# Opening order, zero matmuls and load queues of a fused attention and MLP-mixer kernel

## The chip, the cores and the metric

The kernel runs on one core of one Trainium2 chip. The metric is the device time of one execution in microseconds; all times below are microseconds unless another unit stands beside them. The core has a matmul engine (PE), three engines for elementwise work (DVE, ACT, POOL), and SP, which here only issues transfers. Each works through its own queue in order and waits on semaphores for the others.

## The reference

Four batches of 8 heads, 768 positions and head size 64 go through attention with a sliding window of 128 and four sink keys, and the result through one block of an MLP-mixer with `d_tok` 256 and `d_ch` 1536. All inputs are fp32.

```python
keep = is_sink | in_window                    # first 4 keys, or 0 <= query - key < 128
scores = where(keep, (q @ k.T) / sqrt(D), -1e9)
x = (softmax(scores) @ v), heads side by side # [B, 768, 512]
u = x + (relu(x.T @ w_tok1) @ w_tok2).T
out = u + relu(u @ w_ch1) @ w_ch2
```

## The kernel before

**Tiling.** The 32 heads form eight groups of four: g = 0 to 7, two groups to a batch. Work is cut into named operations, and the names are used in this document. `Lq2.0`, `Lk2.0`, `Lv2.0` load q, k and v of group 2. q and k come as bf16 through a casting transfer issued by POOL; v comes as fp32 through a plain transfer issued by SP and is cast on POOL by `Cv2` into the tile `va`. `Tq2.0` and `Tk2.0` are 32x32 block transposes on DVE that bring q and k into the form the scores need. `SC2.0`, `SC2.1`, `SC2.2` are score matmuls for three pairs of key tiles, `EX` the exponentials on ACT, `MK` the multiplications by a 0/1 mask on DVE, `KZ`, `SK`, `EXK` the same path for the sink keys, `PV2.0` to `PV2.5` the products with v for six tiles of 128 queries, and `XB` the division by the sum, which writes the tile `x_b` and frees the matmul's bank.

The mixer of a batch needs both of its groups: `T1` (with `w_tok1`), `H1` (ReLU), then `T2` (with `w_tok2`), `U` (adds x), `X` and `UTE` (u transposed) or, for half of batch 0, `TT` and `UE`, which make the transposed u directly; then 24 tiles of `C1` (with `w_ch1`), `V` (ReLU), `C2` in three quarters of the inner dimension at a time (with `w_ch2`), `O` (adds u) and the store `ST`. In a name such as `C10.03` the first digit after the operation is the batch.

**Order.** The instructions are written out in an order that a small planner in the kernel computes, `order_of` (line 65). It gives each operation an assumed duration, an assumed landing time for transfers, and picks on each engine what can start first, priorities breaking ties. The list `FIRST` (line 19) gives priorities and engines to the operations of the opening, that is groups 0 and 1 and the first mixer up to the first channel matmuls. The order on each engine is then fixed; only semaphores decide the times.

**What the edit touches.** Group 0's q and k are loaded in two pieces (`PIECES`, line 321): the first piece of each as fp32 by SP, cast by `Ck0.0` on DVE and `Cq0.0` on ACT (lines 345 to 353), the second by casting transfers on POOL (lines 354 to 357). On SP, v of groups 0 and 1 follows. `weight` (line 724) issues the weights on POOL: `tok1`, `tok2`, four pieces of `ch1`, two of `ch2`. v of groups 2 and 3 is held back by a semaphore until the piece `ch1.3` has landed (`gate`, line 366). The buffers for q and k are two deep (`bfp`, line 187), those for raw v three deep (`stage`, line 186), so later loads also wait for their buffers. POOL handles its casts and its transfers in one queue: a load that stands behind a cast waits with it.

**Zero matmuls.** Where the planner sees PE idle before the time `Filler.until` (line 766), it puts in matmuls of the zero tile `warm` into a free bank (lines 110 to 118 and 763 to 774), each 128x512. The tile itself is zeroed on DVE (line 247).

**Masks.** For the pairs listed in `PEM` (line 320) the mask is added on PE by two matmuls of `ident` with `mneg`, and no `MK` follows.

Of the kernel before, what the change touches and what calls it, by code (L numbers as in the profile page):

```python
# [19 lines left out]
MK0.00:D UE0.03:A PV1.3:P vs1:G XB0.1:D SK1:P C10.03:P C10.02:P Tq0.1:D Lv0.0:S Tk1.0:D PV1.5:P XB1.2:D  # L20
EX1.20:A Lk0.1:G blk:G SC1.02:P SC1.00:P SC1.22:P Lq0.1:G Tq0.0:D V0.01:D XB0.3:D first:G vsink:D Lk1.0:G
PV0.0:P EX0.11:A va:G Lk0.0:S V0.02:A T10.014:P zero:D Lq0.0:S XB0.2:D Cq0.0:A MK1.0256:D ident:G Wch2.1:G
T10.104:P Wtok2:G Cv1:G Wch1.1:G MK1.10:D MK0.0256:D T10.114:P EX0.10:A EX0.21:A mnegs:D KZ1:D EX1.00:A SK0:P
C10.00:P EX1.01:A XB1.0:D EX0.01:A MK0.10:D Tk0.1:D EX0.00:A Lq1.0:G Cv0:G PV0.1:P T10.004:P TT0.01:P SC1.12:P
EX1.21:A XB0.5:D MK0.20:D ones:D XB0.0:D V0.00:A H10.00:A Wch1.0:G SC1.10:P SC1.20:P Wch2.0:G PV0.2:P Ck0.0:D
PV1.0:P EX0.20:A PV1.1:P H10.01:A XB1.4:D KZ0:D H10.10:A Tk0.0:D Wch1.3:G rest:G SC0.20:P MK1.00:D H10.11:D
UE0.02:A TT0.00:P UE0.01:A T10.110:P EX1.11:A Lv1.1:S Tq1.0:D PV0.5:P EX1.10:A vsl:G EXK0:A PV1.2:P mneg:G
EXK1:A Wch1.2:G V0.03:D PV0.4:P SC0.22:P SC0.10:P SC0.00:P SC0.02:P PV1.4:P T10.100:P kz:D first1:D SC0.12:P
Wtok1:G TT0.02:P PV0.3:P T10.010:P UE0.00:A XB0.4:D C10.01:P Lv1.0:S TT0.03:P T10.000:P
# [10 lines left out]
class Op:  # L40


    n = 0

    def __init__(self, name, engines, emit, deps=(), pri=0, rows=False, take=(), free=(), land=0.0, dear=None):
        self.name, self.engines, self.emit = name, engines, emit
        self.deps, self.pri, self.rows = [d for d in deps if d is not None], pri, rows
        self.take, self.free, self.land, self.dear = take, free, land, dear or {}
        self.dmas = 1 if land else 0
        self.far = 0.0  # L50
        self.begin = self.end = self.engine = self.made = None
        Op.n += 1
        self.seq = Op.n
# [11 lines left out]
def order_of(ops, slots, filler):  # L65
# [3 lines left out]
    dma_free, rows = {"SP": 1.9, "POOL": 3.4, "ACT": 1.9}, False  # L69
# [8 lines left out]
    def start(op, e):  # L78
        t = free_at[e]
        for d in op.deps:  # L80
            t = max(t, d.end + lag(d, op, e))
        if op.take:
            for kind in {p.kind for p in op.take}:
                n = sum(p.kind == kind for p in op.take)
                t = max(t, sorted(banks[kind])[n - 1])
        if op.dmas:
            t = max(t, flying[e][-9 + op.dmas])
        if e == "PE" and op.rows != rows:
            t += 0.095
        return t  # L90

    while waiting:
        best = None
        ready = [o for o in waiting if all(d.end is not None for d in o.deps)]
        per = {}
        for o in ready:
            at = {e: start(o, e) for e in o.engines}
            soonest = min(at[e] + o.engines[e] + o.dear.get(e, 0) for e in at)
            for e, t in at.items():
                if t < INF and t + o.engines[e] + o.dear.get(e, 0) <= soonest + 1e-9:  # L100
                    per.setdefault(e, []).append((t, o))
        for e, c in per.items():
            first = min(t for t, _ in c)
            t, o = min(((t, o) for t, o in c if t <= first + 0.2), key=lambda x: (x[1].pri, -x[1].far, x[1].seq))
            if best is None or t < best[0]:
                best = (t, e, o)
        if best is None:
            raise RuntimeError("stuck: " + ", ".join(o.name for o in waiting[:20]))
        t, e, o = best
        idle = t - free_at["PE"] - 0.3  # L110
        kind, i = min(((k, i) for k in banks for i in range(slots[k])), key=lambda x: banks[x[0]][x[1]])
        if e == "PE" and filler.until > t and idle > 0.3 and banks[kind][i] < free_at["PE"] - 0.3:
            f = filler.make(kind, i, int(idle / 0.22) + 1)
            f.begin, f.engine = free_at["PE"], "PE"
            f.end = banks[kind][i] = f.begin + f.engines["PE"]
            done.append(f)
            rows = False
            t = max(t, f.end + 0.095 * (o.rows != rows))
        o.begin, o.engine = t, e
        free_at[e] = t + o.engines[e]  # L120
        if e == "PE":
            rows = o.rows
        if o.land:
            dma_free[e] = max(dma_free[e], t + (2.5 if e == "POOL" else 1.4)) + o.land
            o.end = dma_free[e] + 0.9
            flying[e] += [o.end] * o.dmas
        else:
            o.end = free_at[e]
        for p in o.take:
            p.slot = min(range(len(banks[p.kind])), key=lambda i: banks[p.kind][i])  # L130
            banks[p.kind][p.slot] = INF
        for p in o.free:
            p.left -= 1
            if p.left == 0:
                banks[p.kind][p.slot] = free_at[e] + 0.07
        done.append(o)
        waiting.remove(o)
# [12 lines left out]
def kernel(  # L150
# [144 lines left out]
    def c_vsink(e):  # L295
        nc.vector.memset(vsink, 0.0)  # L296
# [23 lines left out]
    PEM = ((1, 2),)  # L320
# [9 lines left out]
    def load_ops(g, deps, vdeps, pri, gate=None):  # L330
# [6 lines left out]
        for n, (w, c) in enumerate([(w, c) for c in range(C) for w in "qk"]):  # L337
# [7 lines left out]
            if g == 0 and c == 0:  # L345
                def plain(e, w=w, src=src):
                    raws[w] = stage.tile([P, R, D], FP32, name="raw_" + w, bufs=1)
                    nc.sync.dma_start(out=raws[w], in_=src)

                def cast(e, w=w, bf=bf):  # L350
                    copy_on[e](bf(), raws[w])
                o = op(f"L{w}{g}.{c}", ("SP", 0.46), plain, [], pri + n, land=land)
                o = op(f"C{w}{g}.{c}", {"ACT": act(R * D), "DVE": dve(R * D, 2)}, cast, [o], pri)
            else:
                def casting(e, src=src, bf=bf):
                    nc.gpsimd.dma_start(out=bf(), in_=src)
                o = op(f"L{w}{g}.{c}", ("POOL", 0.56), casting, deps + (prev.dt[w] if prev else []), pri + n, land=land)
            G.load[w].append(o)
        parts = 2 if g == 1 else 1
        for x in range(parts):  # L360
# [7 lines left out]
            G.load["v"].append(op(f"Lv{g}.{x}", ("SP", 0.46), vv, vdeps, pri + 2, land=GH * S * D * 4e-6 / BWV / parts))  # L368


    def attention(g, xb, base):
# [31 lines left out]
        veng = {"POOL": 1.02e-3 * N}  # L403
        G.cv = [op(f"Cv{g}", veng, castv, G.load["v"] + [c_va_op] + old, -5 if g < 2 else base + 2)]

        def sinkkeys(e):
# [5 lines left out]
        G.kz = op(f"KZ{g}", ("DVE", 0.12), sinkkeys,  # L412
                  G.dt["k"] + [c_kz_op, c_blk_op] + ([prev.sk] if prev else []), base + 1)
# [42 lines left out]
        def masks(u, ex):  # L456
# [3 lines left out]
            for lo, hi, m in ((0, 256, mfirst), (256, 512, mrest)) if u == 0 else ((0, 512 if u == 1 else 384, mrest),):  # L460
# [4 lines left out]
                r.append(op(f"MK{g}.{u}{lo}", ("DVE", dve(4 * (hi - lo), 2)), mask, ex + [c_first_op, c_rest_op], base + u))  # L465
# [237 lines left out]
    c_ident_op = op("ident", ("POOL", 0.6), c_ident, (), -200)  # L703
# [4 lines left out]
    o_vs = op("vsink", ("DVE", 1.2), c_vsink, (), -140)  # L708
# [6 lines left out]
    for o in groups[0].load["v"] + groups[1].load["v"]:  # L715
        o.deps += groups[1].load["k"][-1:]
    o_vsl = op("vsl", ("POOL", 2.6), c_vsink_load, [o_vs], -150, land=0.2)
    o_vsl.dmas = 4
    c_vsink_op = op("vs1", ("POOL", 0.6), c_vsink_one, [o_vs, o_vsl], -60)
# [4 lines left out]
    def weight(key, dst, src, deps, pri, run):  # L724

        def emit(e):
            w_ops[key].made = nc.gpsimd.dma_start(out=dst, in_=src)
        w_ops[key] = op("W" + (key if isinstance(key, str) else f"{key[0]}.{key[1]}"), ("POOL", 0.9), emit, deps, pri, land=dst.shape[0] * dst.shape[1] / 16 * run * 1e-3)
        return w_ops[key]

    weight("tok1", w_tok1, moe_w_tok1.rearrange("(t p) n -> p t n", p=P), [groups[0].load["v"][0]], -40, 60)
    weight("tok2", w_tok2, moe_w_tok2.rearrange("(t p) n -> p t n", p=P), [groups[1].load["v"][0]], -40, 135)
    qf = DCH // 4
    c1w = [weight(("ch1", i), w_ch1[:, :, ts(i, qf)], moe_w_ch1.rearrange("(t p) n -> p t n", p=P)[:, :, ts(i, qf)],
                  [groups[1].load["v"][0]], -40 + i, 78) for i in range(4)]
    c2src = moe_w_ch2.rearrange("(t p) n -> p t n", p=P)
    weight(("ch2", 0), w_ch2[:, 0:8], c2src[:, 0:8], [c1w[0]], -30, 96)
    weight(("ch2", 1), w_ch2[:, 8:12], c2src[:, 8:12], [c1w[0]], -29, 96)
# [5 lines left out]
    for b in range(B):  # L744
        batches[b].x = X(batches[b - 2].u if b >= 2 else [])
        for a in range(GB):
            g = GB * b + a
            if g >= 2:
                deps = [c1w[3]] if g < 4 else []
                load_ops(g, deps, deps + groups[g - 2].cv, 1000 * b - 700, c1w[3] if g < 4 else None)  # L750
# [12 lines left out]
    class Filler:  # L763


        until = 36.0

        @staticmethod
        def make(kind, i, n):
            def emit(e):  # L770
                t = psum[kind][i].tile([P, 512], FP32, name="ps_warm", tag="b")
                for _ in range(n):
                    nc.tensor.matmul(t, warm[:, 0:P], warm, start=True, stop=True)  # L773
            return Op("dummy", {"PE": 0.22 * n}, emit)
# [37 lines left out]
```

## Time and profile before

| | us |
|---|---|
| median of 6 runs | 220.1 (218.75 to 221.13) |
| profiled execution, its own time | 219.4 |
| span of its instructions | 217.7 |
| PE busy | 202.9 (93%) |
| DVE busy | 132.5 (61%) |
| ACT busy | 101.6 (47%) |
| POOL busy | 34.2 (16%) |
| chain that ended last: PE | 87% of the span |

The span runs from the first to the last instruction of the program; the execution's own time holds 1.7 more around it. Times in views of the trace count from the start of the span. In a line of the merged timeline stand the start, the length, the engine, the source line, the operation, what it writes and reads, how many instructions were merged, and in brackets the engine's idle time before it and what ended that. A line of the stretches view holds the stretch, its length, the busy time and number of instructions of PE, PE's weight loads, DVE, ACT and POOL, the granted PE clock, the share of the DMA engines and GB/s by bytes as written. A line on a transfer ends with its size and the time from issue to landing.

### The profile page before, as it was taken

Reading aid. Unit: us, or ns where it says so; the run is one execution under the profiler, and the core shown is the slowest. Engines: PE = TensorE matmul, PEld = TensorE weight load, DVE = VectorE, ACT = ScalarE, POOL = GpSimd, SP = SyncE. Lnnn points to the kernel's source line nnn. Section 1 sums busy time; section 2 is a strip of 40 time slices with the busy share of each in tenths; the row PEclk is TensorE's granted clock in tenths of the full one; section 3 lists DMA queues with packets and bytes.
Section 4 is the critical chain, followed back from the end, with each engine's and each line's share of the span. In section 5 each row is a group of like instructions: output and inputs, shape, how many; then the busy total and the mean of one; then the engine's idle time right before and its main releaser. Section 6 shows DMA issues by size and latency. Waiting matters only on the chain.

```text
span 217.7 us, 4148 instructions
## 1 busy us (share of the span) xinstructions
PE 202.9 (93%) x1744; PEld 116.1 (53%) x1764; DVE 132.5 (61%) x232; ACT 101.6 (47%) x170; POOL 34.2 (16%) x57
## 2 busy tenths in 40 slices
PE   0995999999989999998999999999999999999993
PEld 0442577655546564546765544566755545555552
DVE  7658895259669999999998812589664122001131
ACT  2116765553496511599925320799514301753300
POOL 7919810002260220012000000000000000000000
PEclk9999699999999999999999999999999999999999
DMA  6996999999999955193001013100001113001122
GB/s 175 229 218 90 204 203 197 204 210 230 220 219 235 255 144 118 53 144 76 3 0 48 0 59 114 72 3 3 0 0 51 48 50 114 32 2 48 48 97 99
DMA packets 36243, 23.49 MB, mean 108 GB/s; under 512 B 26112, under 2 KB 31232, under 8 KB 36224
## 3 DMA queue, kind: packets, MB, share of 16 engines
q0 software_dynamic: 7616, 9.85, 26.5%
q1 hardware_dynamic: 28608, 13.37, 25.2%
q8 instruction: 14, 0.23, 0.4%
q14 instruction: 5, 0.04, 0.1%
HBM read 26.77 MB, written 6.29 MB: 152 GB/s over the span
## 4 chain that ended last, share of the span: by engine, by line
PE 87%; DVE 7%; ACT 3%; issue 1%; DVEq 0%
PE ps_v L645 28%; PE ps_w L667 28%; PE ps_s L435 6%; PE ps_warm L773 5%; PE ps_h L560 4%; PE ps_u L612 4%; PE ps_o L511 3%; DVE pT L463 3%; ACT pT L452 2%; PE ps_o L516 2%; PE ps_ut L622 2%; PE ps_o L508 2%; PE ps_k L489 1%; DVE kz L407 1%; DVE vsink L296 1%
## 5 line engine op out<-in xcount | busy, mean ns | idle before, releaser
L645 PE MATMUL ps_v<-uT,w_ch 128*128 128x384 bf16 x384 | 68.0, 326 | 0.7 <-ACT uT L227 0.5
L667 PE MATMUL ps_w<-w_ch,v 128*128 128x512 bf16 (+1 forms) x287 | 65.1, 370 | 0.6
L231 ACT ACTIVATE v<-ps_v 128x384 bf16<-128x384 f32 x86 | 42.1, 493 | 45.0 <-PE ps_v L645 33.9
L452 ACT ACTIVATE pT<-ps_s 128x1024 bf16<-128x1024 f32 (+1 forms) x48 | 43.3, 953 | 28.9 <-PE ps_s L435 26.1
L645 PEld LDWEIGHTS <-w_ch 128*128 128x128 bf16 x384 | 36.4, 98 | 25.4 <-issue 1.4
L677 DVE TENSOR_TENSOR o<-ps_w,u_sb 128x512 f32<-128x512 f32 (+1 forms) x25 | 16.8, 670 | 51.4 <-PE ps_w L667 49.4
L667 PEld LDWEIGHTS <-v 128*128 128x128 bf16 x300 | 28.7, 98 | 29.6 <-issue 0.2
L463 DVE TENSOR_TENSOR pT<-pT,mrest 128x1024 bf16<-128x1024 bf16 (+2 forms) x23 | 22.0, 960 | 3.9 <-ACT pT L452 3.7
L617 DVE TENSOR_TENSOR u_sb<-ps_u,x_b 128x512 bf16<-128x512 f32 x24 | 15.1, 682 | 10.8 <-PE ps_v L645 5.1
L532 DVE TENSOR_TENSOR x_b<-ps_o,rc 128x256 bf16<-128x256 f32 (+1 forms) x45 | 19.9, 442 | 1.5
L226 POOL CAST va<-raw_v 128x1536 bf16<-128x1536 f32 x8 | 11.8, 1473 | 47.0 <-DMA raw_v<-in_v_dram 26.9
L435 PE MATMUL ps_s<-qT,kT 32*128 32x256 bf16 (+1 forms) x384 | 17.7, 269 | 1.5 <-ACT pT L452 1.4
L385 DVE STREAM_TRANSPOSE qT<-qb 128x768 uint32<-128x768 uint32 (+1 forms) x9 | 16.4, 1873 | 1.8 <-DMA qb<-in_q_dram 1.8
L511 PE MATMUL ps_o<-va,pT 128*128 128x65 bf16 x192 | 16.7, 197 | 0.7 <-DVE h L233 0.3
L385 DVE STREAM_TRANSPOSE kT<-kb 128x768 uint32<-128x768 uint32 (+1 forms) x9 | 16.8, 1885 | 0.0
L773 PE MATMUL ps_warm<-warm 128*128 128x512 bf16 x43 | 11.8, 433 | 5.2 <-DVE warm L247 5.1
L435 PEld LDWEIGHTS <-kT 32*128 32x128 bf16 x384 | 9.9, 94 | 11.1 <-issue 9.9
L511 PEld LDWEIGHTS <-pT 128*128 128x128 bf16 x192 | 14.0, 99 | 3.0 <-DVE h L233 0.6
L516 PE MATMUL ps_o<-va,pT 128*128 128x65 bf16 x160 | 15.1, 195 | 0.0
L227 ACT ACTIVATE uT<-ps_ut 128x512 bf16<-128x512 bf16 (+1 forms) x13 | 7.3, 564 | 13.0 <-PE ps_ut L622 12.6
L560 PE MATMUL ps_h<-x_b,w_tok 128*128 128x256 bf16 x96 | 12.1, 273 | 0.0
L516 PEld LDWEIGHTS <-pT 128*128 128x128 bf16 x160 | 11.6, 99 | 0.8 <-issue 0.4
(60 smaller groups left out, 136.0 us busy)
## 6 DMA issues: line engine op xcount, KB each, us to landing
out_dram<-o SPq DMA_DIRECT2D x23, 256.0 KB, 2.0
raw_v<-in_v_dram SPq DMA_DIRECT2D x7, 768.0 KB, 11.7
kb<-in_k_dram POOLq DMA_DIRECT2D x7, 384.0 KB, 10.2
qb<-in_q_dram POOLq DMA_DIRECT2D x7, 384.0 KB, 7.9
w_ch<-in_moe_w_ch_dram POOLq DMA_DIRECT2D x4, 384.0 KB, 8.7
w_ch<-in_moe_w_ch_dram POOLq DMA_DIRECT2D x1, 1024.0 KB, 18.5
raw_v<-in_v_dram SPq DMA_DIRECT2D x2, 384.0 KB, 12.5
w_tok<-in_moe_w_tok_dram POOLq DMA_DIRECT2D x2, 384.0 KB, 5.6
```

What stands on the lines that cost most here:

```text
L231: nc.scalar.activation(o, i, AF.Relu)
L385: nc.vector.transpose(G.T[w].rearrange("p s x -> p (s x)").bitcast(UINT32).rearrange("p (i r) -> p r i", i=Q)[:, r], G.bf[w][:, r].bitcast ...
L435: nc.tensor.matmul(bank[h][:, at:at + w], G.T["k"][r, ts(kt, P), db], G.T["q"][r, ds(kt * P, w), db], start=not pem and db == 0, stop=db = ...
L452: nc.scalar.activation(o, i, AF.Exp, scale=scale)
L463: nc.vector.tensor_tensor(out=t, in0=t, op=ALU.mult, in1=m[:, 0:hi - lo].rearrange("p (o x) -> p o x", o=1).to_broadcast([P, GH, hi - lo]))
L511: nc.tensor.matmul(ps[:, h], G.pT[qt // 2][:, h, ds(256 * (qt % 2), P)], G.va[:, h, qt], start=(qt < 2 and h == 0), stop=(h == GH - 1 and ...
L516: nc.tensor.matmul(ps[:, h], G.pT[kt // 2][:, h, ds(256 * (kt % 2) + P, P)], G.va[:, h, kt], start=False, stop=(h == GH - 1), skip_group_c ...
L532: nc.vector.tensor_tensor(out=xb.tile[:, ds(q0, n), c0:c0 + W].rearrange("p n (h d) -> p n h d", h=GH), in0=ps[:, :, :, 0:D], in1=rc.to_br ...
L560: nc.tensor.matmul(p.tile, w_tok1[:, t, ts(tt, P)], xb.tile[:, t, ds(a * W, W)], start=(t == 0), stop=(t == NT - 1))
L645: nc.tensor.matmul(ps, w_ch1[:, c, ts(ft, P)], M.uT[hf][:, c], start=(c == 0), stop=(c == NC - 1))
L667: nc.tensor.matmul(p.tile, M.v1t[hf][:, ft, ts(st % NH, P)], w_ch2[:, ft, ds(lo, n)], start=(ft == 0), stop=(ft == NF - 1))
L773: nc.tensor.matmul(t, warm[:, 0:P], warm, start=True, stop=True)
```

## The change

- **Order list.** `FIRST` is replaced by another list. On DVE `warm` comes first; the zeroing of `vsink` goes to ACT; all casts of group 0's q and k go to ACT; the cast of v of group 0 goes from POOL to DVE.
- **First loads.** Both pieces of group 0's q and k are plain fp32 transfers on SP, in the order k piece 1, q piece 0, k piece 0, q piece 1, ahead of v. On POOL the memsets and selects for `va`, `blk`, `ident` and `mneg` come ahead of the casting loads of group 1's k and q. The ones in `vsink` are written before its four small transfers instead of after them.
- **Masks.** The pair (0, 0) joins `PEM`, so group 0's first mask is added on PE.
- **Zero matmuls.** The first block has 24 of 128x512 instead of 38. Later gaps before time 29.0 of the plan are filled with 128x128 ones, 19 in three places, instead of six of 128x512 in two.
- **Weights.** `tok1` waits by a semaphore for v of group 0; the other weights follow it in a row on POOL, with the cast of v of group 1 between the second and the third piece of `ch1`, and all come ahead of q and k of groups 2 and 3 (which are planned in this order too: q2, q3, k2, k3). The eight pieces had come as `ch1.1`, `ch1.0`, `ch1.3`, `ch1.2`, `ch2.1`, `ch2.0`; now they come in the order of their numbers.
- **Planner.** It now keeps DVE and POOL operations marked `port` apart in time, holds some operations behind the placing of others (`follows`), and has other assumed durations. So the order of the later batches changes as well: for instance `Tq4.0` stands on DVE directly behind `XB2.3` instead of behind `XB3.5` and `O0.40`, the scores `SC2.0` stand two `C1` tiles sooner on PE, and `Tq7.0` stands ahead of `U2.0` instead of behind `UTE2.4`.

```diff
-    dma_free, rows = {"SP": 1.9, "POOL": 3.4, "ACT": 1.9}, False
+    dma_free, rows = {"SP": 1.9, "POOL": 6.0, "ACT": 1.9}, None
...
+        for d in op.follows:
+            t = max(t, d.begin + d.engines[d.engine])
...
+        if e in op.port:
+            t = max(t, port)
...
-        idle = t - free_at["PE"] - 0.3
+        idle = t - free_at["PE"] - (1.0 if rows is None else 0.15)
...
-        if e == "PE" and filler.until > t and idle > 0.3 and banks[kind][i] < free_at["PE"] - 0.3:
-            f = filler.make(kind, i, int(idle / 0.22) + 1)
+        if e == "PE" and filler.until > t and idle > 0.15 and banks[kind][i] < free_at["PE"] - 0.2:
+            f = filler.make(kind, i, idle, rows is None, o.rows)
...
     def c_vsink(e):
-        nc.vector.memset(vsink, 0.0)
+        nc.scalar.activation(vsink.rearrange("p g h x -> p (g h x)"), warm[:, 0:1].to_broadcast([P, NG * GH * D1]), AF.Copy)
...
-    PEM = ((1, 2),)
+    PEM = ((0, 0), (1, 2))
...
-            if g == 0 and c == 0:
-                def plain(e, w=w, src=src):
-                    raws[w] = stage.tile([P, R, D], FP32, name="raw_" + w, bufs=1)
-                    nc.sync.dma_start(out=raws[w], in_=src)
+            if g == 0:
+                def plain(e, w=w, c=c, src=src):
+                    raws[w, c] = stage.tile([P, R, D], FP32, name=f"raw_{w}{c}", bufs=1)
+                    nc.sync.dma_start(out=raws[w, c], in_=src)
...
+            if g in (2, 3):
+                o.follows = [w_ops["ch2", 1]]
...
-        veng = {"POOL": 1.02e-3 * N}
+        veng = {"POOL": 0.96e-3 * N}
+        if g < 2:
+            veng |= {"DVE": dve(N, 2), "ACT": act(N)}
...
-    for o in groups[0].load["v"] + groups[1].load["v"]:
-        o.deps += groups[1].load["k"][-1:]
...
+    for o in groups[1].load["q"] + groups[1].load["k"]:
+        o.deps += [c_ident_op, o_mneg, c_blk_op]
...
             w_ops[key].made = nc.gpsimd.dma_start(out=dst, in_=src)
+            if key == "tok1":
+                behind_of(w_ops[key].made, groups[0].load["v"][0])
...
-                load_ops(g, deps, deps + groups[g - 2].cv, 1000 * b - 700, c1w[3] if g < 4 else None)
+                load_ops(g, [], deps + groups[g - 2].cv, 1000 * b - 700, c1w[3] if g < 4 else None)
...
-        until = 36.0
+        until = 29.0
...
-        def make(kind, i, n):
+        def make(kind, i, us, first, rows):
+            n = int(us / 0.33) if first else int(us / 0.058)
+
             def emit(e):
                 t = psum[kind][i].tile([P, 512], FP32, name="ps_warm", tag="b")
                 for _ in range(n):
-                    nc.tensor.matmul(t, warm[:, 0:P], warm, start=True, stop=True)
-            return Op("dummy", {"PE": 0.22 * n}, emit)
+                    if first:
+                        nc.tensor.matmul(t, warm[:, 0:P], warm, start=True, stop=True)
+                    elif rows:
+                        nc.tensor.matmul(t[:, 0:P], warm[0:Q, 0:P], warm[0:Q, 0:P], start=True, stop=True, tile_position=(0, 0))
+                    else:
+                        nc.tensor.matmul(t[:, 0:P], warm[:, 0:P], warm[:, 0:P], start=True, stop=True)
+            return Op("dummy", {"PE": us}, emit)
```

## The prediction

> **What bounds the kernel now.** The page gives PE 93% of the span and 87% of the chain of waits, so I read the merged timeline to see which stretches PE does not set itself. There are two. In the opening, up to the first channel matmul:
>
> ```profile
> 5.07 10.17 PE L773 MATMUL ps_warm<-warm 128*128 128x512 bf16 x38 [5.07 <-DVE warm L247]
> ...
> 9.57 2.08 DVE L385 STREAM_TRANSPOSE qT<-qb 128x384 uint32<-128x384 uint32 x2 [1.76 <-DMA qb<-in_q_dram]
> ...
> 15.17 0.64 PE L435 MATMUL ps_s<-qT,kT 32*128 32x256 bf16 x16
> ...
> 17.58 1.59 POOL L727 DMA_DIRECT2D w_tok<-in_moe_w_tok_dram  x2
> ...
> 18.37 2.33 DVE L407 TENSOR_TENSOR kz<-kT,blk 128x32 bf16<-128x32 bf16 x1
> ...
> 37.46 7.96 PE L645 MATMUL ps_v<-uT,w_ch 128*128 128x384 bf16 x48
> ```
>
> The scores' operands are ready at 11.6 (9.57 + 2.08), yet PE is busy with 38 zero matmuls until 15.2; kz, usually 0.19, takes 2.33. From 37.46 PE runs to 214.35 (204.66 + 9.69, its last row) nearly without idle.
>
> The second view is the DMA, by stretches (last two columns: share, GB/s), then POOL's timeline, and the answer for one load of q:
>
> ```profile
> 17.00:19.00 2.00, 1.48 (x20) 0.69 (x16) 1.73 (x2) 1.98 (x3) 2.00 (x3) 1.00 0.09 14
> 19.00:21.00 2.00, 0.24 (x2) 0.11 (x2) 2.00 (x2) 1.11 (x2) 2.00 (x3) 1.00 0.74 83
> 21.00:34.00 13.00, 13.00 (x183) 8.73 (x182) 11.93 (x25) 8.04 (x11) 6.37 (x10) 0.87 1.29 204
> 34.00:49.00 15.00, 14.87 (x104) 9.08 (x105) 5.83 (x12) 8.27 (x17) 0.00 (x0) 1.00 1.15 203
> 49.00:64.00 15.00, 14.26 (x100) 7.17 (x99) 11.22 (x11) 8.13 (x15) 6.48 (x7) 1.00 1.25 223
> ```
> ```profile
> 52.77 1.47 POOL L226 CAST va<-raw_v 128x1536 bf16<-128x1536 f32 x1 [22.56 <-DMA raw_v<-in_v_dram]
> 56.43 1.47 POOL L226 CAST va<-raw_v 128x1536 bf16<-128x1536 f32 x1 [2.18 <-DMA raw_v<-in_v_dram]
> 60.03 1.47 POOL L226 CAST va<-raw_v 128x1536 bf16<-128x1536 f32 x1 [2.13 <-DMA raw_v<-in_v_dram]
> 61.44 1.06 POOL L356 DMA_DIRECT2D qb<-in_q_dram  x2
> ```
> ```profile
> qb<-in_q_dram POOLq DMA_DIRECT2D x1, 384.0 KB, 6.9
> ```
>
> From 21 to 64 the transfers never rest. The casts of v2, v3, v4 wait for their landings, 3.6 apart, and the loads of q4 and k4 stand behind the cast of v4 on POOL, so q4 lands at 61.4 + 6.9 = 68.3. Nobody waits for it: its transpose stands late on DVE.
>
> ```profile
> 80.98 2.07 DVE L385 STREAM_TRANSPOSE qT<-qb 128x768 uint32<-128x768 uint32 x1
> ```
>
> **What the Trainium skill says.** "DMA: Bandwidth & Descriptors", Queues, rings and completion order: an engine switches between queues packet by packet. The trace agrees: v in small pieces took about 21 (31.4 to 52.7) beside casting loads with larger packets, 3.6 alone. "SBUF — State Buffer", Who interferes with whom: a VectorE instruction with two SBUF inputs and a GpSimd instruction that reads SBUF lock each other out. The kz row agrees: it ends at 20.70, with POOL's cast of v1 (19.16 to 20.65). "TensorE: Matmul & The Clock Gate", Part 1: after an idle window of about 3.4 us the clock halves, and that much activity restores it. Agrees: the first zero matmuls stand 0.43 apart, later ones 0.21; the granted clock falls to 0.74 in 20 to 25.
>
> **The change part by part: the opening.** (1) `warm` becomes DVE's first instruction, ready at 1.31 + 0.27 = 1.6 instead of 5.0, and 24 zero matmuls follow: 9 x 0.43 + 15 x 0.21 = 7.0, done at 8.7. (2) Four plain reads of 384 KB go first on SP. The first two landed at 4.5 and 5.4; POOL's casting loads no longer run beside them, since va, blk, ident and mneg (0.41 + 0.83 + 1.18 + 1.24 from 1.31) now stand ahead of these: at about 1.1 each the others land at 6.7 and 7.8. (3) ACT takes the zeroing of vsink, 1.9 by its 128x1024 and 128x768 rows (1.02, 0.84), done at 4.0, hidden before the first landing; DVE loses 1.79. Four casts at 0.84 keep up with the landings, the last ends at 8.7, its transpose (1.1) at 9.8. Scores start at 9.9, 5.3 earlier. (4) From there DVE sets the pace. Lk1 is issued at 5.0 instead of 3.3 and lands at about 10.7; then two transposes of 2.07, masks 0.96 + 1.2 + 2 x 0.65 + 1.2, kz 0.19, the cast of v0 moved from POOL (0.95, twice the 0.48 of the 768-wide cast), nine x_b outputs (6 x 0.55 + 3 x 0.88): 15.9, with about 1.5 for waits on PE and on POOL's cast of v1: 28.1. The two masks saved by the second PE mask (2 x 0.69) cost two matmul pairs. From DVE's last output to the first channel matmul took 3.3 before (34.14 to 37.46): 31.4, and with 0.8 for delays that the rows don't show about 32.2, **5.2 earlier**. The 19 short zero matmuls between cost PE about 1.1, in its own gaps; uncovered they cost that, or double at half clock.
>
> **After the opening.** All operations remain, but their order on each engine changes. I laid both orders out with the rows' durations (channel matmuls 0.65, quarters of the second product 0.86, scores 0.57 and 0.45, x_b 0.55, masks 0.61 to 1.14, transposes 2.0, u 0.62), each engine in its own order. For before this gives 176.0 from the first channel matmul to PE's end; the trace has 176.9. For after it gives 178.5 if every load is there: PE's waits add to 10.6 instead of 6.7, mostly for banks that DVE must empty (PV3.2 to PV3.5 2.0, PV5.2 1.05, X2.0 to X2.2 1.4, since the transpose Tq7.0 of 2.07 now stands ahead of U2.0). So the opening's 5.2 shrinks to **-2.6**.
>
> **The wait it adds.** Tq4.0 moves on DVE from behind all x_b of group 3 to directly behind XB2.3. When does DVE reach it? Scores of group 2 stood 22.1 behind the first channel matmul and now stand two channel tiles (1.3) sooner: 52.8; the first V on DVE behind them (0.5 + 0.45 + 0.65 + 0.2) at 54.6; from there to Tq4.0 2 x 0.53 + 2 x 0.62 + masks 3.24 + 4 x 0.55 = 7.7, and 0.9 for the cast of v3 on the shared port: **63.2**. When is q4 there? The weights now start when v0 lands, about 15.5 by the bytes queued before it, not at 17.58; v1's rest beside them costs 0.3. The casting stream moves 1.7 forward, but v2, gated on the last ch1 piece, which is now fourth instead of third, starts where it did and has less time beside that stream: v4 lands 1.4 earlier, 58.5, its cast ends at 60.0, and with the same 6.9 q4 lands at **66.9**. I take 66.7. Bounds: the whole lull of 17 to 21 saved (3.2) and the best q row (issue to landing 4.6) give 62.8; nothing saved gives 68.3. Behind Tq4.0 on DVE wait XB2.4, XB2.5, the masks of group 3; behind those PE's T11.000 and PV3.0. DVE is 94% busy over 70 to 80, so the stall passes on whole: 66.7 - 63.2 = **+3.5**.
>
> **Sum:** -2.6 + 3.5 = +0.9: span 218.6, that execution 219.4 + 0.9 = 220.3. It stood 0.7 under the median 220.1, so I forecast 221.0. A later opening changes nothing up to 3.5: DVE would then only wait less for q4. Moving weights ahead of q2 and k2 costs nothing, since those were already last on POOL's queue; of the gates, only that of tok1 on v0 is new, and behind it on POOL stand all weights and the cast of v1.
>
> **Rivals.** *A, the gain gets through*: q4 lands by 63.2; for it, the best row of 4.6 and the lull; against, v5 and v6 still fill the queue then, as before. 220.1 - 2.6 = 217.5. *B, slower*: v0, which now has four full reads ahead of it, lands no earlier than 17.6, so the weights and hence v4 gain nothing; q4 at 68.3 gives -2.6 + 5.1: 222.6; it decides from a landing of q4 later than 66.9. For it: v in small pieces yields to Lk1 and Lq1. Against: v0 landed at 15.2 with the same bytes ahead. *C, the opening does not get shorter*: PE at half clock after 8.7, with gaps of about 1, or locked ports; likely by 1 or 2, and hidden by the wait for q4.
>
> **Numbers.** Forecast with C (q4 between 65 and 67.5): 0.50, its own range 219.4 to 221.9. A: 0.20. B: 0.30. A measurement of this kernel can tell about 0.5%, 1.1 us, from no change. Faster by that (below 219.0): A nearly whole and a little of the forecast, 0.20; within: 0.43; slower (above 221.2): B and the upper part of the forecast, 0.37. Two in ten left out on both sides: 217.8 to 223.3.
>
> **What would show it.** Scores at about 10, first channel matmul at 31 to 33, PE's zero matmuls done by 9. Then a DVE transpose of qT near 63 to 67 whose idle time before is ended by the DMA of qb, 2 to 4 long, and T11.000 waiting for x_b. The steps are wrong if that wait is under 1, if v0 lands after 17, or if PE waits for w_ch.

## The result

The changed kernel takes 220.31 (median of 35 runs, 219.5 to 224.46), the kernel before, run in between, 220.68 (median of 72, 218.31 to 221.82). The ratio is 1.001, with a 95% interval from 0.9994 to 1.0025: no difference that can be measured. The forecast was 221.0; the profiled execution has a span of 218.5 where 218.6 was forecast.

Executions of one kernel differ in how long PE ran at half clock in them, and the ratios leave out executions more than 1.5% above the fastest of the same kernel; below, times are therefore also compared at equal granted clock.

**The opening.** From the merged timeline of the changed kernel, taken engine by engine:

```profile
1.26 7.53 PE L791 MATMUL ps_warm<-warm 128*128 128x512 bf16 x24 [1.26 <-DVE warm L254]
...
9.00 1.13 DVE L395 STREAM_TRANSPOSE qT<-qb 128x384 uint32<-128x384 uint32 x1
...
10.18 0.52 PE L447 MATMUL ps_s<-qT,kT 32*128 32x256 bf16 x8 [1.38 <-DVE kz L419]
...
12.67 2.09 DVE L395 STREAM_TRANSPOSE kT<-kb 128x768 uint32<-128x768 uint32 x1 [2.28 <-DMA kb<-in_k_dram]
...
15.58 1.60 POOL L739 DMA_DIRECT2D w_tok<-in_moe_w_tok_dram  x2 [5.71 <-DMA raw_v<-in_v_dram]
16.49 1.03 PE L447 MATMUL ps_s<-qT,kT 32*128 32x256 bf16 x8
...
33.91 7.96 PE L657 MATMUL ps_v<-uT,w_ch 128*128 128x384 bf16 x48
```

The zero matmuls end at 8.8 and the scores start at 10.18, 5.0 earlier than before. DVE then waits 2.28 for k1. Eight score matmuls of one form take 0.52 at 10.18 and 1.03 at 16.49: PE is at half clock. The first channel matmul starts at 33.91, 3.55 earlier than before (37.46).

The stretches view of the changed kernel, cut where the clock changes (the granted clock is the third column from the right):

```profile
9.13:12.54 3.41, 2.36 (x32) 1.53 (x32) 1.26 (x3) 1.61 (x3) 0.74 (x3) 1.00 1.16 215
12.54:15.95 3.41, 2.99 (x27) 1.38 (x26) 3.28 (x4) 2.76 (x5) 0.37 (x1) 0.50 1.23 222
15.95:19.37 3.42, 3.42 (x26) 1.84 (x25) 3.42 (x3) 2.04 (x3) 3.42 (x4) 0.50 1.30 178
19.37:22.78 3.41, 3.41 (x39) 2.38 (x37) 1.89 (x7) 1.72 (x3) 3.41 (x5) 0.50 1.21 194
22.78:26.20 3.42, 3.42 (x55) 2.11 (x53) 2.58 (x8) 3.02 (x4) 2.83 (x5) 1.00 1.31 203
```

Three stretches of 3.41 in a row at half clock, 10.2 in all; the kernel before has one, 22.39 to 25.80.

**After the opening.** POOL's timeline, the answer for the load of q4, and DVE's timeline of the changed kernel:

```profile
54.21 1.49 POOL L233 CAST va<-raw_v 128x1536 bf16<-128x1536 f32 x1 [2.10 <-DVE kT L395]
57.68 1.94 POOL L233 CAST va<-raw_v 128x1536 bf16<-128x1536 f32 x1 [1.98 <-DMA raw_v<-in_v_dram]
59.57 1.06 POOL L363 DMA_DIRECT2D qb<-in_q_dram  x2
```
```profile
qb<-in_q_dram POOLq DMA_DIRECT2D x1, 384.0 KB, 7.5
```
```profile
58.21 1.95 DVE L475 TENSOR_TENSOR pT<-pT,mrest 128x1024 bf16<-128x1024 bf16 x1
...
67.08 2.08 DVE L395 STREAM_TRANSPOSE qT<-qb 128x768 uint32<-128x768 uint32 x1 [1.15 <-DMA qb<-in_q_dram]
```

The cast of v4 ends at 59.6, q4 is issued behind it and lands at 67.06, and DVE, which had come to `Tq4.0` at 65.93, waits 1.15 for it. The page of the changed kernel puts this load into the chain that ended last, where none of q4 stood before:

```profile
PE 71%; DMA 11%; DVE 10%; ACT 3%; issue 2%; SPq 1%; POOLq 0%; POOL 0%
PE ps_w L679 23%; PE ps_v L657 23%; PE ps_s L447 6%; DMA raw_v<-in_v_dram 5%; PE ps_h L572 4%; PE ps_u L624 4%; DVE pT L475 3%; DMA qb<-in_q_dram 3%; DMA raw_q<-in_q_dram 3%; DVE x_b L544 3%; DVE qT L395 2%; ACT pT L464 2%; PE ps_ut L634 2%; PE ps_o L523 2%; PE ps_o L520 2%
```

PE's last row starts at 204.70 and takes 10.55, so from the first channel matmul to PE's end pass 215.25 - 33.91 = 181.34, where the kernel before took 176.89 (37.46 to 214.35). The opening gains 3.55 and the rest gives back 4.45: a span 0.9 longer by these starts and ends, 0.8 by the page.

### The profile page after: what moved, and what is told of

The parts are those of the page before. It is cut to its first block, busy times and chain, and to the rows that moved or that the text cites. A ratio compares the mean times of both kernels' runs of the same rounds, so it can differ in the third digit from the quotient of the medians.

```text
span 218.5 us, 4156 instructions
## 1 busy us (share of the span) xinstructions
PE 206.0 (94%) x1748; PEld 117.7 (54%) x1767; DVE 127.7 (58%) x227; ACT 107.1 (49%) x176; POOL 32.5 (15%) x54
## 4 chain that ended last, share of the span: by engine, by line
PE 71%; DMA 11%; DVE 10%; ACT 3%; issue 2%; SPq 1%; POOLq 0%; POOL 0%
PE ps_w L679 23%; PE ps_v L657 23%; PE ps_s L447 6%; DMA raw_v<-in_v_dram 5%; PE ps_h L572 4%; PE ps_u L624 4%; DVE pT L475 3%; DMA qb<-in_q_dram 3%; DMA raw_q<-in_q_dram 3%; DVE x_b L544 3%; DVE qT L395 2%; ACT pT L464 2%; PE ps_ut L634 2%; PE ps_o L523 2%; PE ps_o L520 2%
## 5 line engine op out<-in xcount | busy, mean ns | idle before, releaser
L238 ACT ACTIVATE v<-ps_v 128x384 bf16<-128x384 f32 x85 | 41.4, 493 | 50.8 <-PE ps_v L657 40.0
L475 DVE TENSOR_TENSOR pT<-pT,mrest 128x2048 bf16<-128x2048 bf16 (+2 forms) x22 | 22.2, 1020 | 1.0 <-ACT pT L464 0.7
L447 PE MATMUL ps_s<-qT,kT 32*128 32x256 bf16 (+1 forms) x384 | 20.5, 280 | 2.1 <-DVE kz L419 1.4
L447 PEld LDWEIGHTS <-kT 32*128 32x128 bf16 x384 | 11.1, 97 | 12.2 <-issue 9.5
L233 POOL CAST va<-raw_v 128x1536 bf16<-128x1536 f32 x7 | 10.8, 1543 | 44.3 <-DMA raw_v<-in_v_dram 24.8
L234 ACT ACTIVATE uT<-ps_ut 128x512 bf16<-128x512 bf16 (+1 forms) x14 | 7.9, 567 | 10.0 <-PE ps_ut L634 8.3
L624 PE MATMUL ps_u<-h,w_tok 128*128 128x512 bf16 x44 | 12.2, 378 | 0.4 <-ACT uT L234 0.2
```

The source lines that it names most:

```text
L238: nc.scalar.activation(o, i, AF.Relu)
L447: nc.tensor.matmul(bank[h][:, at:at + w], G.T["k"][r, ts(kt, P), db], G.T["q"][r, ds(kt * P, w), db], start=not pem and db == 0, stop=db = ...
L475: nc.vector.tensor_tensor(out=t, in0=t, op=ALU.mult, in1=m[:, 0:hi - lo].rearrange("p (o x) -> p o x", o=1).to_broadcast([P, GH, hi - lo]))
L624: nc.tensor.matmul(ps, w_tok2[:, tt, ts(st, P)], M.h1t[:, tt], start=(tt == 0), stop=(tt == NTOK - 1))
```

## The experiments

To move single operations without the planner rearranging all others, the experiments give every engine its order as a list; the planner then only assigns banks and merges the engines' lists. An experiment's line numbers are thereby some 70 higher.

```diff
+ORDER = """
...
+"""
...
-        ready = [o for o in waiting if all(d.end is not None for d in o.deps + o.follows)]
+        heads = {v[0] for v in lists.values() if v}
+        ready = [o for o in waiting if o.name in heads and all(d.end is not None for d in o.deps + o.follows)]
...
         done.append(o)
+        lists[e].pop(0)
         waiting.remove(o)
```

In the fences on `ORDER`, the lists are cut to the operations around a move, or are told in words. The theory: the opening really is shorter; what eats the gain is the order behind it, and the landing of q4, which holds `Tq4.0` at about 67 however early DVE comes to it. The rivals: the loads hold everything anyway; or the gain in the opening is not real; or q4 counts for nothing.

### New opening, old order

The lists of the changed kernel up to the first channel matmul, then those of the kernel before (with `Tq4.0` late on DVE).

```diff
-ORDER: opening of the changed kernel, then its own order
+ORDER: opening of the changed kernel, then the order of the kernel before
```

> The opening of the changed kernel (all loads, casts, fillers and operations up to the first channel matmul), followed on every engine by the order of the kernel before. Theory (the opening is really 3.5 shorter, and what gives the gain back is the order behind it, together with the transpose of q4 standing early on DVE): first channel matmul at about 34, from there to PE's end about 177 to 178 instead of 181.3, span about 215, time about 216.5 (2% below before). Rival 'the loads hold the end' (v2 to v5, q4, k4 come no earlier, so a shorter opening only waits elsewhere): 219.5 to 220.5, with new waits of DVE or PE for a DMA. Rival 'the opening's gain is not real': no change either, but the first channel matmul is then near 37.

Six executions gave 213.59, 216.81, 217.22, 217.78, 219.43, 220.16 (median 217.5; the kernel before beside it 220.69), at granted clocks of 1.0, 0.976, 0.976, 0.968, 0.958, 0.953. The profiled one is the first. PE's timeline:

```profile
15.63 0.63 PE L517 MATMUL ps_s<-qT,kT 32*128 32x256 bf16 x8
...
31.75 7.96 PE L727 MATMUL ps_v<-uT,w_ch 128*128 128x384 bf16 x48
...
198.11 10.55 PE L749 MATMUL ps_w<-w_ch,v 128*128 128x512 bf16 x59
```

At full clock, the opening ends at 31.75, 5.7 earlier than before, and from there to PE's end it takes 208.66 - 31.75 = 176.91, as before (176.89). The whole gain comes through, so the loads do not hold the end and the gain is real. What was not expected is the scatter, and that it follows the clock. The opening of 31.75, with the same zero matmuls as in the changed kernel (33.91), also shows what the three half-clock stretches cost there: 2.2.

### Old opening, new order

```diff
-ORDER: opening of the kernel before, then its own order
+ORDER: opening of the kernel before, then the order of the changed kernel
```

> The reverse: the opening and the loads of the kernel before, followed on every engine by the order of the changed kernel. Here DVE reaches the transpose of q4 about 69.5, after its landing (68.3), so there is next to no wait for it. Theory (the order itself costs 2 to 3.3, with the wait on q4 apart): first channel matmul at 37.5, to PE's end 179 to 180, span about 220.5, time 222.5 to 224. Rival 'the order costs nothing, the wait for q4 is all of what is given back': 220 to 221.

Median 224.43, ratio 1.0165 (1.012 to 1.021). PE's timeline, and DVE's:

```profile
39.62 6.66 PE L715 MATMUL ps_v<-uT,w_ch 128*128 128x384 bf16 x40
...
208.70 10.55 PE L737 MATMUL ps_w<-w_ch,v 128*128 128x512 bf16 x59
```
```profile
70.58 0.42 DVE L602 TENSOR_TENSOR x_b<-ps_o,rc 128x256 bf16<-128x256 f32 x1
70.92 2.07 DVE L455 STREAM_TRANSPOSE qT<-qb 128x768 uint32<-128x768 uint32 x1
```

From the first channel matmul to PE's end pass 219.25 - 39.62 = 179.63, 2.7 more than in the order before, with no wait for q4 at all. That part is as expected: the order costs by itself. The opening came out 2.1 later than the 37.5 expected, and the time above the 222.5 to 224 expected; here the clock is at half from 21 to 28, two stretches of 3.4 instead of one.

### The transpose of q4 late, the load of q4 early

Two single moves in the changed kernel.

```diff
 D: XB2.2 MK2.20 XB2.3
-   Tq4.0
    XB2.4 XB2.5
...
    O0.20 O0.30
+   Tq4.0
    Tk4.0 U1.0
```

> The changed kernel with one operation moved: the transpose of q4 stands on DVE directly ahead of that of k4, behind all x_b of group 3. Theory: the wait of 1.15 goes, and so do the 2.08 of the transpose from the stretch in which PE waits for DVE's x_b; about 1 comes back where the first transposes of u wait for DVE. 1.5 to 2.5 faster than the changed kernel: about 218.2. Rival 'only the wait counts': 1.15 faster, 219.2. Rival 'DVE's order there does not set the end': 220.3.

Median 221.66 of 22, ratio to the kernel before 0.998 (0.9944 to 1.0015): no gain, the expected 1.5 to 2.5 were missed. In the trace, with the same three half-clock stretches as the changed kernel, two waits stand in the place of the one removed (PE's timeline):

```profile
73.01 0.28 PE L590 MATMUL ps_o<-vsink,pk 128*128 128x260 bf16 x1 [1.16 <-DVE x_b L614]
...
80.43 0.40 PE L704 MATMUL ps_ut<-ident,u_sb 128*128 128x128 bf16 x4 [1.00 <-DVE u_sb L699]
```

The second is the price foreseen for the transposes of u; the first was there before (0.89). The two executions at full clock are the fastest, 218.13 and 218.26, where the changed kernel at full clock takes 219.62 to 220.07 (four runs): there the gain is 1.6, as expected. At 0.977 the kernel takes 219.76 to 221.37 and the changed one 219.72 to 220.5, no gain.

```diff
 G: Lk3.0 Cv2
+   Lq4.0
    Cv3 Cv4
-   Lq4.0
    Lq5.0 Lk4.0 Lk5.0
```

> The changed kernel with one DMA issue moved: the load of q4 stands on POOL ahead of the cast of v3 instead of behind the cast of v4, so it is issued near 52 instead of 59.6 and should land near 59 to 61; v3 and v4 then land about 1.9 later (56 and 59.5), where DVE and PE do not need them yet. Theory: DVE's wait of 1.15 before the transpose of q4 is gone and the end moves by it: 219.2, no more. Rival 'the landing of q4 holds much more than the trace's 1.15': 217 or less. Rival 'nothing': 220.3, with the 1.15 turning up as another wait.

Six executions from 216.48 to 224.35, median 221.94, ratio 0.9887 (0.9793 to 0.9981, from two runs). At a clock of 0.976 it took 219.6, where the changed kernel takes 219.72 to 220.5 at 0.977; at full clock 216.48 against 219.62 to 220.07. So, by one execution each, the wait for q4 is worth about 0.5 with three half-clock stretches, near the theory, and over 3 with none, as the rival had it; neither had made it depend on the clock. That calls for kernels in which the clock is held.

### Holding the clock

The opening of the changed kernel with the old order behind it, and other zero matmuls. First 30 in front instead of 24:

```diff
-            n = int(us / 0.33) if first else int(us / 0.058)
+            n = 30 if first else int(us / 0.058)
```

> New opening and old order behind it, with 30 zero matmuls instead of 24 ahead of the scores, so that PE has no idle 1.4 there. Theory 1 (a clock window with idle time on PE lets the clock fall, and the idle stretch at 8.8 to 10.2 is the one that did it): the granted clock stays full from about 7 on in every run, time 213.6 each time. Theory 2 (what lets it fall is what fills PE from 10 to 18: scores and zero matmuls on 32 rows, and the gap ahead of the scores of group 1): it still falls for one or more windows of 3.4 us in most runs, time 214 to 220 as without the six.

213.6, 213.64, 216.67 and 217.44, at clocks of 0.998, 1.0, 0.992 and 0.976: it held in two of four. Then also wide ones in the three gaps between the scores:

```diff
-            n = int(us / 0.33) if first else int(us / 0.058)
+            n = Filler.counts.pop(0)
...
-                    if first:
-                        nc.tensor.matmul(t, warm[:, 0:P], warm, start=True, stop=True)
-                    elif rows:
-                        nc.tensor.matmul(t[:, 0:P], warm[0:Q, 0:P], warm[0:Q, 0:P], start=True, stop=True, tile_position=(0, 0))
-                    else:
-                        nc.tensor.matmul(t[:, 0:P], warm[:, 0:P], warm[:, 0:P], start=True, stop=True)
+                    nc.tensor.matmul(t, warm[:, 0:P], warm, start=True, stop=True)
...
+        counts = [30, 2, 3, 7]
```

> As the run before, and the three fillers between the scores are 2, 3 and 7 zero matmuls of 128x512 on 128 rows instead of 6, 7 and 6 of 128x128 on 32 rows. Theory 2: the clock now holds in all or nearly all runs, first channel matmul at 32, time 213.5 to 214.5. If neither kind of zero matmul matters to the clock: 214 to 220, as before.

Median 213.82, ratio 0.971 (0.9668 to 0.9753); five of six lie between 213.55 and 214.06, one at 216.36, and the clock is 1.0 in all; what cost that one 2.5 is not known. This kernel beats both. Two of the stretches in which the changed kernel was at half clock, as they are here, and PE's timeline:

```profile
12.54:15.95 3.41, 3.41 (x31) 1.40 (x31) 3.18 (x4) 3.18 (x5) 0.26 (x1) 1.00 1.24 222
15.95:19.37 3.42, 3.42 (x38) 1.67 (x35) 3.42 (x3) 2.19 (x3) 3.42 (x4) 1.00 1.15 162
```
```profile
16.21 1.69 PE L861 MATMUL ps_warm<-warm 128*128 128x512 bf16 x7
...
31.64 7.96 PE L727 MATMUL ps_v<-uT,w_ch 128*128 128x384 bf16 x48
```

And 24 in front with the wide ones in the gaps:

```diff
-        counts = [30, 2, 3, 7]
+        counts = [24, 2, 3, 7]
```

> New opening and old order, 24 zero matmuls in front as in the changed kernel, and the three fillers of 2, 3 and 7 on 128 rows. Theory 2 (the fillers on 32 rows and the gap ahead of the scores of group 1 let the clock fall): the clock holds in most runs, 213.6 to 214.5. Theory 1 (the idle stretch ahead of the scores): it falls in most runs, 214 to 220.

213.56, 213.61, 214.01 and 218.53, at 0.998, 0.999, 0.999 and 0.976: held in three of four. Without either it held in one of six, and in 8 of 69 when the other kernels with the changed kernel's zero matmuls are counted in (the changed one 4 of 35, q4's transpose late 2 of 22, q4's load early 1 of 6). So neither of the two theories is right alone: each measure makes a fall rarer, and with both it did not come in six runs. So few runs don't say how much each does, and wide zero matmuls are no sure means: in the last experiment below they stand in the gaps too, with 38 in front and the scores nearly 3 later, and the clock held in 6 of 20.

### The landing of q4, with the clock held

The changed kernel in its own order, with the same zero matmuls (30, 2, 3, 7), and then also with the load of q4 early.

> The changed kernel, its order untouched, with the 30 zero matmuls and the three fillers on 128 rows. Theory (the landing of q4 holds the end of the changed kernel): the opening gets about 2 shorter, first channel matmul at 32, but DVE then waits about 3 for q4 instead of 1.15, and the end stays: 219.5, at most 0.8 faster than the changed kernel. Rival (its end follows its opening): 218 or less.

Median 220.03 of 20, ratio 0.9991 (0.9971 to 1.0012): nothing, with an opening 2.2 shorter. DVE's and PE's timelines show where it went:

```profile
63.12 0.42 DVE L614 TENSOR_TENSOR x_b<-ps_o,rc 128x256 bf16<-128x256 f32 x1
66.51 2.09 DVE L465 STREAM_TRANSPOSE qT<-qb 128x768 uint32<-128x768 uint32 x1 [2.97 <-DMA qb<-in_q_dram]
```
```profile
31.73 7.96 PE L727 MATMUL ps_v<-uT,w_ch 128*128 128x384 bf16 x48
...
69.14 0.83 PE L642 MATMUL ps_h<-x_b,w_tok 128*128 128x256 bf16 x6 [2.06 <-DVE x_b L614]
...
204.15 10.55 PE L749 MATMUL ps_w<-w_ch,v 128*128 128x512 bf16 x60
```

DVE comes to `Tq4.0` at 63.54 and waits 2.97 for q4; behind that, PE waits 2.06 for `x_b`. To PE's end it takes 214.70 - 31.73 = 182.97. The clock was held through the opening, but not behind this wait:

```profile
70.16:73.58 3.42, 3.40 (x40) 1.89 (x29) 3.35 (x8) 1.74 (x3) 0.00 (x0) 0.50 1.14 238
```

That stretch is not what makes the end late: nine of the twenty executions had full clock throughout, and they took 219.41 to 220.52, the eleven others 219.63 to 221.1.

> The run before with the load of q4 ahead of the cast of v3 on POOL as well. Theory: DVE's wait for q4 is gone and the opening's gain comes through, all but the 2.5 to 3 of the new order: 216.3. Rival (q4 does not hold the end): as the run before.

Median 216.76, ratio 0.9847 (0.9794 to 0.9901); three of four lie between 216.35 and 216.81, one at 218.67, for which nothing here gives the reason. From DVE's and PE's timelines:

```profile
63.60 2.07 DVE L465 STREAM_TRANSPOSE qT<-qb 128x768 uint32<-128x768 uint32 x1
```
```profile
32.04 7.96 PE L727 MATMUL ps_v<-uT,w_ch 128*128 128x384 bf16 x48
...
108.71 0.40 PE L704 MATMUL ps_ut<-ident,u_sb 128*128 128x128 bf16 x4 [0.29 <-DVE u_sb L699]
...
201.22 10.55 PE L749 MATMUL ps_w<-w_ch,v 128*128 128x512 bf16 x60
```

The wait is gone, and to PE's end it takes 211.77 - 32.04 = 179.73. So q4 costs 182.97 - 179.73 = 3.24, and the order by itself 179.73 - 176.89 = 2.84. Both together are shown to hold the end; the rival that the end follows the opening is out.

How it holds the end shows when the time from the start of `Tq4.0` to PE's end is taken: 214.70 - 66.51 = 148.19 here with the wait, 211.77 - 63.60 = 148.17 without it, and 215.25 - 67.08 = 148.17 in the changed kernel itself. In the new order DVE sets the pace from this transpose on, and whatever delays it is passed on whole.

### A piece of the order's price

In the last kernel, one more move on DVE:

```diff
 D: XB5.4 XB5.5 Tk6.0 KZ6
-   Tq7.0
    U2.0 U2.1 U2.2 UTE2.0 UTE2.2 U2.3 U2.4 U2.5
+   Tq7.0
    UTE2.4 MK6.00
```

> The changed kernel with wide zero matmuls and q4's load early, and one more operation moved: the second transpose of q of group 7 stands on DVE behind the six outputs U2 (u of batch 2) instead of ahead of them. Theory (part of the 2.8 that the new order costs is this transpose of 2.07 ahead of U2.0, for which PE's transposes X2.0 to X2.2 wait): 1.4 faster than the run without the move (216.8), 215.4. Rival (the wait turns up elsewhere): 216.8.

Median 215.33, 1.43 faster than without the move, as expected. The first outputs u of batch 2 stand at 106.32 instead of 107.92, and PE's waits of 0.29, 0.20 and 0.20 for them are gone. From the scores ahead of these transposes to the second product behind them PE takes 112.10 - 107.51 = 4.59 instead of 113.67 - 107.78 = 5.89, most of the 1.43. DVE's timeline:

```profile
106.32 1.89 DVE L699 TENSOR_TENSOR u_sb<-ps_u,x_b 128x512 bf16<-128x512 f32 x3 [0.45 <-PE ps_u L694]
...
111.09 2.07 DVE L465 STREAM_TRANSPOSE qT<-qb 128x768 uint32<-128x768 uint32 x1
```

Half of the order's 2.84 is this one transpose. The other half was not taken apart.

### One part of the change undone: k1 and q1 beside the plain reads

```diff
-    for o in groups[1].load["q"] + groups[1].load["k"]:
-        o.deps += [c_ident_op, o_mneg, c_blk_op]
...
-G: va blk ident mneg Lk1.0 Lq1.0
+G: Lk1.0 Lq1.0 va blk ident mneg
...
-        counts = [30, 2, 3, 7]
+        counts = [38, 2, 3, 7]
```

> New opening and old order with wide fillers, and one part of the change undone: the casting loads of k1 and q1 stand first on POOL, beside the four plain reads, as in the kernel before (38 zero matmuls in front, since the scores then start later). Theory (the FIFO of plain reads pays only in part, since DVE waits 2.3 for k1 behind it): the last plain read lands about 2 later, near 10, scores start near 12, k1 lands before DVE is through with the transposes of group 0, so its chain loses 2.3 of waiting and gains 2 of lateness: first channel matmul within 0.7 of 31.7, time 213 to 214.6. Rival (the opening follows the first scores): 2 later, 215.8.

Median 217.93 of 20, ratio 0.9934 (0.9884 to 0.9984); 216.15 to 216.49 in the six runs at a clock of 0.998 or more. The rival came nearer: 2.5 later by these six, where it had said 2 (215.8). DVE's and PE's timelines:

```profile
11.90 1.13 DVE L465 STREAM_TRANSPOSE qT<-qb 128x384 uint32<-128x384 uint32 x1 [1.13 <-ACT qb L304]
13.22 2.02 DVE L465 STREAM_TRANSPOSE kT<-kb 128x768 uint32<-128x768 uint32 x1
...
19.44 2.48 DVE L545 TENSOR_TENSOR pT<-pT,mrest 128x2048 bf16<-128x2048 bf16 x1
```
```profile
34.42 7.96 PE L727 MATMUL ps_v<-uT,w_ch 128*128 128x384 bf16 x48
```

k1 no longer makes DVE wait, and its transpose starts only 0.45 later than the 12.77 of the kernel with the wide zero matmuls. But the scores, the exponentials and the mask at 19.44 are later too, the mask by 1.0, and it takes 2.48 instead of 1.20, as it now meets POOL's cast of v1 (18.70 to 20.83, 2.13 long instead of 1.49). So keeping the casting loads from beside the plain reads is worth 2.5 (time) to 2.8 (opening) of the gain, nearly half of it (1.3) through this meeting of mask and cast. The other parts of the opening were not undone one by one.

## Why the prediction was right, and where not

**The total.** The forecast span was 218.6, the profiled one 218.5; but two terms of the sum were off, against each other. And the +0.9 was worked out against one execution of the kernel before: against the median of its executions nothing of it shows (ratio 1.001, at most 1.0025, or 0.6), for the reason at the end of this section.

| term | forecast | profiled run | clock held |
|---|---|---|---|
| opening | -5.2 | -3.55 | -5.7 |
| order behind it | 178.5 - 176.0 = +2.5 | +2.84 | +2.84 |
| start of `Tq4.0` | +3.5 | +1.61 | +3.24 |
| sum | +0.8, taken as +0.9 | +0.9 | +0.4 |

The last column takes the opening from the changed kernel with the wide zero matmuls (31.73 against 37.46), and the 2.84 of both columns is the one measured there. In the profiled run `Tq4.0` starts 67.08 - 33.91 = 33.17 behind the first channel matmul, and 63.60 - 32.04 = 31.56 where q4 comes early: 1.61 later, of which 1.15 are the wait and 0.46 DVE's own later arrival. Two slips stand in the forecast's sums and change it by 0.2 at most: 5.2 less 2.5 is 2.7, not 2.6, and 32.2 + 22.1 - 1.3 is 53.0, not 52.8.

**Opening, steps 1 to 3.** Zero matmuls done at 8.8 (forecast 8.7), landings at 4.05, 5.1, 6.85 and 8.1 (4.5, 5.4, 6.7, 7.8), last transpose ending at 10.1 (9.8), scores at 10.18 (9.9). Right.

**Opening, step 4.** Two errors cancelled. k1 landed at 12.65 instead of 10.7, though its issue began at 4.1 already; the 1.9 show as DVE's wait of 2.28. And DVE's chain from the transpose of k1 to its last output took 12.77 to 28.31 = 15.5 in the kernel with the wide zero matmuls, not 15.9 and 1.5 for waits: the allowance for waits was not used. With the clock held the first channel matmul stood at 31.6 to 32.0, forecast 32.2. That the forecast fits so well is luck in this step. In the profiled run it stood at 33.91. That is rival C, half clock in gaps of PE, said to be likely by 1 or 2 and hidden by the wait for q4: it is 2.2, and it is hidden.

**The wait.** q4 landed at 67.06 (66.9 worked out, 66.7 taken): v0 at 15.3 (15.5), v4 at 57.5 and its cast done at 59.6 (58.5 and 60.0), then 7.5 instead of 6.9. DVE was there at 65.93, not at 63.2; with the clock held, at 63.54. The step that was off for the profiled run is the time at which DVE comes there: 1.7 of it from the later opening, 1.0 from the way from the first channel matmul to there (65.93 - 33.91 = 32.0, forecast 63.2 - 32.2 = 31.0). On that way the mask at 58.21 took 1.95 instead of 0.68 beside POOL's cast, 1.3 for which the forecast had allowed 0.9, and DVE waited 0.42 for PE at 63.87. So the stall was 1.15 instead of 3.5. The forecast had said that a later opening takes nothing from the total up to 3.5, which is what kept it right. That the stall passes on whole was right too: 2.97 on DVE, 3.24 at the end, by the constant 148.2 above.

**Which case it was.** Rival A asked for q4 by 63.2; it came 4 later. Rival B asked for v0 after 17; it came at 15.3. By B's other mark, a landing of q4 later than 66.9, it was met, if barely: 67.06 lies 0.2 beyond, as the load itself took 0.6 longer, but the weights and v4 did gain what B denied them. The mark "2 to 4 long" for the wait was missed in the profiled run, mostly by the half clock, and so was `T11.000` waiting for x_b: it starts at 69.70, right behind the row ahead of it. With the clock held both are there, 2.97 and 2.06.

**What the prediction left out.** It treated the half clock as a delay of the opening only. It is also what makes executions of one kernel differ: a half-clock stretch of 3.41 lowers the granted clock over the span by about 0.008. By the runs (of the kernel before, those beside the experiments):

| granted clock | before | changed | k1 first |
|---|---|---|---|
| 0.997 to 1.0 | 218.03 to 218.84, one 216.61 | 219.62 to 220.07 | 216.15 to 216.49 |
| 0.989 to 0.992 | 219.33 to 220.82 | 220.06 | 217.73 to 217.99 |
| 0.982 to 0.984 | 220.63 to 222.02 | 221.17 | 219.31 to 220.74 |
| 0.974 to 0.977 | | 219.5 to 220.5 | |
| 0.967 to 0.969 | | 220.31 to 221.11 | |
| 0.960 | | 221.19 to 221.89 | |
| 0.946 | | 224.36 and 224.46 | |

The two kernels in which nothing waits for q4 lose between 1 and 2 for each stretch; the changed kernel loses next to nothing for the first three (but for one execution, 221.17), and starts to lose beyond, as it should once the opening is so late that DVE no longer waits for q4 (no trace here shows such a run). At full clock the changed kernel is about 1 slower than the one before; in ordinary runs the two are equal because the kernel before pays for its stretches and the changed one hardly does.

## What to carry to other kernels

When a stretch is shortened, look for the next fixed date behind it: here one load, issued behind a cast on POOL and landing at 67 whatever the opening did, swallowed every gain up to 3. A pin of this kind showed in the scatter of times too: the time of the kernel that waited for q4 hardly followed its own granted clock. And a new order should be paid for separately: the new opening with the old order, and zero matmuls with which the clock held, gave 213.8, 3% below both.

## What the runs showed of the hardware

The clock falls and returns in steps of 3.41 (10.24 in the changed kernel is three). The Trainium skill, "TensorE: Matmul & The Clock Gate", Part 1, says that an idle window of that length halves the clock and that a busy one restores it. The length agrees; the rest does not. The stretch ahead of a fall was not idle: PE was busy 1.63 of it in the kernel before (the fall that the prediction counts as agreeing) and 2.36 in the changed kernel (9.13 to 12.54). And after its fall PE was busy 2.99, 3.42 and 3.41 of 3.41 in three stretches of the changed kernel, mostly with score and zero matmuls on 32 rows in the first two, and stayed at half clock through all three; the measurement decides. The stretch of the kernel before, and one of the changed kernel that kept the clock though PE was busy for less than in the one that lost it:

```profile
18.97:22.39 3.42, 1.63 (x13) 0.70 (x14) 3.42 (x2) 1.55 (x3) 3.42 (x5) 1.00 1.02 133
```
```profile
73.98:77.39 3.41, 2.31 (x36) 1.83 (x33) 3.19 (x11) 0.16 (x1) 1.09 (x1) 1.00 0.95 194
```

The second lies 18 stretches of 3.413 behind the 12.54 at which the clock of that kernel fell, and the first ends where the clock fell, so both are whole stretches of the clock's own grid. So the busy time alone does not decide. That work on few rows counts for less is a guess that fits, and that the clock held more often with wide zero matmuls fits it too, but what exactly is counted stays open.

A casting load of 384 KB took 8.5 from its issue to its landing beside the plain reads (k1, 4.11 to 12.65), and a mask on DVE beside POOL's cast took 1.95 instead of 0.68, with the cast at 1.94 instead of 1.47: both engines lose. The second is what the Trainium skill's "SBUF — State Buffer", Who interferes with whom, says of such a pair. The row of kz in the prediction fits it in its end only: it began at 18.37, 0.8 ahead of POOL's cast, and what held it until the cast began is not shown.
